# Windowed attention, a gated MLP and routed experts on one core: another way to take exponentials in six banks, and a new order

## The chip, the cores and the metric

The kernel runs on one core of a Trainium2 chip. The core has a matrix engine (TensorE: PE in the profile, with PEld for its weight loads), VectorE (DVE), ScalarE (ACT), GpSimd (POOL), and SyncE (SP), which here issues the loads and stores. The engines run their own queues of instructions in order and wait for one another by semaphores. The metric is the device time of one execution in microseconds.

## The reference

Three stages in float32, each fed with the result of the one before. Batch is 4, the sequence 576, the model width 512.

```python
# 1: 8 heads of 64, causal, window of 64 keys
scores = q @ k.T / 8;  masked outside 0 <= row - col < 64
attn = exp(scores - max);  attn / (attn.sum() + 1e-9) @ v
# 2: gated MLP with a product along the sequence
h = maximum(x @ w_in, 0);  u, v = h[..., :512], h[..., 512:]
v_n = (v - mean) / sqrt(var + 1e-6)
x = (u * (w_spatial @ v_n + b_spatial)) @ w_out
# 3: four causal attention experts, the best two of each token
out = sum over chosen e of w_e * softmax(x wq[e] (x wk[e]).T / 8) (x wv[e]) wo[e]
```

## The kernel before, in words

**Planner.** The Python code doesn't write its instructions in a fixed order. It makes nodes: a cost in nanoseconds for each engine that could do it, what it depends on, the buffers that it takes, and a priority. `Planner.run` plays the engines forward in time with these costs, and whenever an engine is free it emits the ready node of the best priority. A node with a choice (a copy, say, on ACT or DVE) goes to the engine that is expected to end it first, with a bias for each engine. So what stands where in the queues follows from tables of numbers at the head of the file: `SWITCH` (a penalty when PE changes between 64-row and 128-row work), `DVE_BIAS`, `POOL_BIAS` and `EFT` (one number for each of the two runs of the planner), and `SHIFT`, which adds an offset to the priority of every unit of work. It runs twice: once for stages 1 and 2 with the preparation of weights for stage 3 ("phase 1", to about 280 us of the trace), once for stage 3 ("phase 2").

**Dummies.** At the start PE multiplies the identity by itself (`heat`), `WARM` times in one go, and then there are `FILL` = 60 single such nodes of the lowest priority, which the planner emits wherever PE has nothing else that is ready. All are executed; in the profile they are `bank<-ident`, two matmul instructions each.

**Attention of stage 1** (`a_couple`). The 48 groups (batch, pair of heads, third of the sequence) go in 24 couples. A couple fills two banks of PSUM, one for each head of its pairs: PE computes scores in 64-row matmuls (`bank<-kt,qa`, or `ut,qa` and `vt`); DVE scales them, adds the mask and takes the row's least value (L546, three pieces of 128x128; signs are turned, so that the least stands for the greatest score); ACT takes three exponentials with the least as bias, each with the sum of the row accumulated (L552); DVE adds a constant to the sums (L568) and takes the reciprocal (L570); POOL, DVE (L560) or ACT (L558) multiplies; PE transposes (L564, `ident,pa`); ACT or DVE copies to `pt`; PE multiplies by the values (`pt,vt` or `pt,woh`).

**Gated MLP.** Weights come as 64-bit floats and are turned into float32 and split in a high and a low part: DVE shifts and joins words (L686 to L696), ACT or POOL copies the high part, POOL or DVE subtracts it to get the low part (`w<-y,w` at L357). The activations `x` are split in the same way (`xh`, `xl`, and `xt` for the last 64 tokens of a batch). A product takes three matmuls, high by high, high by low, low by high. The v half of the first layer is made of 128x512 matmuls (`w,xh`), the u half of 128x288 (`xh,w`). Then come the product along the sequence with `wsp_h` and `wsp_l`, the gate (L835), and `w_out`.

**Stage 3.** For each batch and pair of experts: `qs`, `kd`, `kz` copies, scores with the mask on DVE (L1207), exponentials on ACT (L1218), normalisation together with the gate on DVE or POOL (L1222), transposes on PE (L1238), copies to `pg` on ACT or DVE (L344, L348), products with the values and with `wo` and copies to `ot` for the store.

A helper issues all plain matmuls (L333), another the copies (L344 for ACT, L346 for POOL, L348 for DVE), a third the subtractions (L357).

Of the kernel before, what the change touches and what calls it, by code (L numbers as in the profile page):

```python
# [26 lines left out]
SWITCH = 107920.0  # L27
A_BIAS = 10098.0
C_BIAS = 162315.0
DVE_BIAS = (1136.0, 1147.0)  # L30
POOL_BIAS = (1131.0, 1068.0)
WARM = 8
FILL = 60
LOADS = (-130000, -120000, -43801, -5807, 14591, 18276, 34028)
EFT = (636.0, 778.0)
# [233 lines left out]
def attn_gmlp_moe_kernel(ctx: ExitStack, tc: tile.TileContext, kq0, qT, kT, v, w_in, wspT, b_sp, w_outT,  # L269
# [228 lines left out]
    def a_couple(n0):  # L498
# [25 lines left out]
        def vap(x, vi, e):  # L524
            b, p, _ = grp[x]
            c = e * 64 + (0 if b else (p % 2) * 128)
            return hv[x][:, vi, c:c + 64]

        def s_mm(_):
            for j in range(3):  # L530
                for x, e in ((0, 0), (1, 1), (1, 0), (0, 1)):
                    win = max(0, 64 * (3 * grp[x][2] + j - 1))
                    mm(bank[e][HALF[x], j * 128:(j + 1) * 128], qap(x, j, e), kap(x, win, e))

        def mask(j):
            return MASK[tuple(int(3 * g + j > 0) for _, _, g in grp)]

        S_N[n0] = S_N[n0 + 1] = top = N((PE, 816), s_mm, kn + [Q_N[n0], Q_N[n0 + 1], S_N.get(n0 - 1)], alloc=bank, use=hk, prio=prio,
                                        form=1)
        done = []  # L540
        for ps, pt in zip(bank, pts):
            pa, mx, ps2 = r_pa.new(), r_mx.new(), r_at.new()

            def s_top(_, ps=ps, pa=pa, mx=mx):
                for j in range(3):
                    dve.tensor_tensor_reduce(out=pa[:, j, :], in0=ps[:, j * 128:(j + 1) * 128],  # L546
                                             in1=mask(j), scale=-0.125, scalar=3.0e38,
                                             op0=ALU.add, op1=ALU.min, accum_out=mx[:, j, 0:1])
# [24 lines left out]
            done.append(N(on_copy(384), lambda e, pt=pt, ps2=ps2: copy(e, pt.t.rearrange("p a b -> p (a b)"), ps2[:, :384]),
                          [a], use=[ps2, pt], prio=prio))
# [554 lines left out]
    def c_gate(b):  # L1129
# [6 lines left out]
        def gt():  # L1136
            return ga[:, 0]
# [16 lines left out]
        tt, tr_ = dve.tensor_tensor, dve.tensor_reduce
        n1 = N_(90, lambda: tr_(out=m1(0), in_=lg, axis=AX.X, op=ALU.max), LG_N[b], [ex, ga, gb])
# [5 lines left out]
        nf = N_(0, lambda: None, [n2, n3, n4])  # L1161
# [14 lines left out]
    def unit(b, pr, e, I):  # L1176
# [38 lines left out]
        if len(parts) == 2:  # L1215
            tops = [N((DVE, 70), lambda e: dve.tensor_reduce(out=mc[:m, 0:1], in_=mc[:m, 0:2], axis=AX.X, op=ALU.min), tops, use=[mc], prio=prio)]
# [211 lines left out]
```

## Time and profile before

| | us |
|---|---|
| time before, median of 2 runs (447.51 to 447.91) | 447.71 |
| the profiled execution: its time | 448.94 |
| its span in the trace | 447.1 |
| busy in the span: PE | 438.9 (98%), 3962 instructions |
| DVE | 310.9 (70%), 1241 |
| ACT | 293.1 (66%), 926 |
| POOL | 107.4 (24%), 154 |
| granted clock of PE, mean | 1.0 |

The profiled execution is longer than its span by 448.94 - 447.1 = 1.84 us, which lie ahead of its first and behind its last instruction. Times of a row in order of time are the start from the beginning of the span and the duration; "x6" counts the instructions that the row joins. Matmuls are pipelined, so their durations overlap and the pitch (start to start) says what one costs. What stands in brackets is idle time ahead of the row and the instruction that ended it.

### The profile page before, as it was taken

How to read it: one execution, taken by the hardware profiler on the slowest of the kernel's cores; microseconds unless marked ns; L12 is line 12 of the kernel's file. 1: busy time of each engine (PE TensorE's matmuls, PEld its weight loads, DVE VectorE, ACT ScalarE, POOL GpSimd, SP SyncE). 2: the span in 40 equal slices, each digit the busy share in tenths (PEclk: the TensorE clock that was granted, in tenths of full speed). 3: DMA queues.
4: the chain of work that ended last, by engine and by line, in shares of the span. 5: the costliest groups of instructions: out<-in, count | busy, mean ns of one | idle time of the engine just before them, and what ended most of it. 6: DMA issues, size and time to landing. Idle time of an engine off the chain costs nothing.

```text
span 447.1 us, 10829 instructions
## 1 busy us (share of the span) xinstructions
PE 438.9 (98%) x3962; PEld 396.0 (89%) x3962; DVE 310.9 (70%) x1241; ACT 293.1 (66%) x926; POOL 107.4 (24%) x154
## 2 busy tenths in 40 slices
PE   8999999999999999999999999999999999999996
PEld 7977899989899879998899999789899978897875
DVE  4989989962875988024544556998697987787650
ACT  4989989662676969203322346987675978777863
POOL 4335782400310126000200251610031011011110
PEclk9999999999999999999999999999999999999999
DMA  7994837140242605003001000000010001000114
GB/s 280 281 330 122 251 101 221 45 140 0 64 138 64 179 7 144 0 1 95 1 1 48 0 1 1 1 2 1 1 48 25 1 2 48 0 2 25 71 53 160
DMA packets 31079, 33.10 MB, mean 74 GB/s; under 512 B 1905, under 2 KB 24689, under 8 KB 31026
## 3 DMA queue, kind: packets, MB, share of 16 engines
q1 hardware_dynamic: 31026, 32.41, 23.4%
q8 instruction: 31, 0.51, 0.5%
q14 instruction: 22, 0.18, 0.1%
HBM read 27.68 MB, written 4.72 MB: 72 GB/s over the span
## 4 chain that ended last, share of the span: by engine, by line
PE 87%; DVE 6%; ACT 4%; issue 2%; POOL 1%; POOLq 0%; ACTq 0%; DVEq 0%
PE bank L333 79%; PE bank L1238 5%; PE bank L564 3%; DVE p L1207 1%; ACT pa L552 1%; DVE qs L357 1%; POOL p L1222 1%; DVE p L1222 1%; ACT p L1218 1%; DVE pa L546 0%; ACT pa L558 0%; DVE pa L560 0%; DVE kz L357 0%; ACT pg L344 0%; ACT kd L344 0%
## 5 line engine op out<-in xcount | busy, mean ns | idle before, releaser
L333 PE MATMUL bank<-xh,w 128*128 128x288 f32 x512 | 109.6, 298 | 0.0
L333 PEld LDWEIGHTS bank<-xh,w 128*128 128x128 f32 x512 | 84.1, 188 | 0.9 <-DVE st L767 0.2
L333 PE MATMUL bank<-xl,w 128*128 128x288 f32 x256 | 75.3, 294 | 0.0
L333 PE MATMUL bank<-w,xh 128*128 128x512 f32 (+1 forms) x256 | 64.7, 342 | 0.2 <-ACT pt L344 0.2
L552 ACT ACTIVATE pa<-pa,mx 128x128 f32<-128x128 f32 x144 | 55.9, 400 | 5.4 <-DVE mx L546 5.4
L333 PEld LDWEIGHTS bank<-xl,w 128*128 128x128 f32 x256 | 48.2, 188 | 0.4
L333 PEld LDWEIGHTS bank<-w,xh 128*128 128x128 f32 x256 | 43.2, 188 | 5.7 <-ACT pt L344 0.5
L1218 ACT ACTIVATE p<-p,mc 128x128 f32<-128x128 f32 (+4 forms) x72 | 41.8, 582 | 8.4 <-DVE mc L1207 7.7
L1222 POOL TENSOR_SCALAR p<-p,mc,fx 128x256 f32<-128x256 f32 (+4 forms) x26 | 17.1, 658 | 111.3 <-DVE mc L1221 52.2
L333 PE MATMUL bank<-w,xl 128*128 128x512 f32 (+1 forms) x128 | 43.2, 338 | 0.0
L333 PE MATMUL bank<-wsp_h,vh 128*128 128x288 f32 x128 | 38.6, 302 | 0.0
L333 PE MATMUL bank<-wsp_h,vl 128*128 128x288 f32 x128 | 37.7, 295 | 0.0
L333 PE MATMUL bank<-wsp_l,vh 128*128 128x288 f32 x128 | 37.7, 294 | 0.0
L1207 DVE CUSTOM_DVE_ANT_0 p<-bank,cmask 128x128 f32<-128x128 f32 (+4 forms) x72 | 33.2, 482 | 5.2 <-PE bank L333 4.2
L770 POOL TENSOR_TENSOR st<-st,nhalf 128x1 f32<-128x1 f32 (+1 forms) x20 | 12.3, 615 | 98.7 <-DVE st L769 98.7
L344 ACT ACTIVATE pg<-bank 128x128 f32<-128x128 f32 (+4 forms) x71 | 29.1, 440 | 5.2 <-PE bank L1238 4.7
L546 DVE CUSTOM_DVE_ANT_0 pa<-bank,mask 128x128 f32<-128x128 f32 x120 | 28.4, 284 | 5.9 <-POOL mx L415 4.1
L1238 PE MATMUL bank<-ident,p 128*128 128x128 f32 x192 | 30.1, 278 | 1.5 <-POOL p L1222 0.7
L333 PE MATMUL bank<-kd,qs 128*128 128x128 f32 (+5 forms) x96 | 30.5, 335 | 0.0
L552 ACT ACTIVATION_READ_ACCUMULATOR pa<-pa,mx 128x1 f32 x144 | 28.6, 199 | 0.0
L333 PE MATMUL bank<-kz,qs 128*128 128x128 f32 (+5 forms) x96 | 28.4, 313 | 0.0
L835 DVE TENSOR_TENSOR y<-bank,ut 128x288 f32<-128x288 f32 x24 | 10.9, 454 | 24.9 <-PE bank L333 24.9
(209 smaller groups left out, 1083.4 us busy)
## 6 DMA issues: line engine op xcount, KB each, us to landing
vt<-in_v_dram SPq DMA_DIRECT2D x12, 512.0 KB, 4.9
qa<-in_qT_dram SPq DMA_DIRECT2D x44, 96.0 KB, 3.8
out_dram<-ot SPq DMA_DIRECT2D x15, 256.0 KB, 2.0
y<-in_w_in_dram SPq DMA_DIRECT2D x7, 512.0 KB, 7.3
kt<-in_kT_dram SPq DMA_DIRECT2D x12, 288.0 KB, 5.0
y<-in_w_outT_dram SPq DMA_DIRECT2D x4, 512.0 KB, 4.5
y<-in_wspT_dram SPq DMA_DIRECT2D x2, 576.0 KB, 4.2
vt<-in_kq_dram SPq DMA_DIRECT2D x2, 384.0 KB, 4.4
```

The costliest lines, as they stand in the source:

```text
L333: pe.matmul(o, lhsT, rhs, start=start, stop=stop)
L344: act.activation(o, i, AF.Copy)
L357: engs[e].tensor_tensor(out=o, in0=a, in1=hi.bitcast(F32), op=ALU.subtract)
L546: dve.tensor_tensor_reduce(out=pa[:, j, :], in0=ps[:, j * 128:(j + 1) * 128], in1=mask(j), scale=-0.125, scalar=3.0e38, op0=ALU.add, op1=A ...
L552: act.activation(pa[:, j, :], pa[:, j, :], AF.Exp, bias=mx[:, j, 0:1], scale=-1.0, accum_out=mx[:, j, 1:2])
L564: pe.transpose(ps2[:, j * 128:(j + 1) * 128], pa[:, j, :], ident)
L770: a = N((POOL, 464), lambda e: pool.tensor_tensor(out=st[:m, 9:10], in0=st[:m, 8:9], in1=nhalf[:m], op=ALU.pow), [n1], use=[st])
L835: dve.tensor_tensor(out=o, in0=ps[:, :HS], in1=u[:, d, tk], op=ALU.mult)
L1207: dve.tensor_tensor_reduce(out=P[:, a0:a1], in0=ps[:, :w], in1=msk, scale=-0.125, scalar=3.0e38, op0=ALU.add, op1=ALU.min, accum_out=mc[:, ...
L1218: a = N((ACT, 284 + 0.87 * L), lambda e: act.activation(P[:m, :L], P[:m, :L], AF.Exp, bias=mc[:m, 0:1], scale=-1.0, accum_out=mc[:m, 2:3]) ...
L1222: a = N({POOL: 328 + 0.832 * L, DVE: 90 + 0.52 * L}, lambda e: engs[e].tensor_scalar(P[:, :L], P[:, :L], mc[:, 3:4], fx[:, I, ev:ev + 1], ...
L1238: pe.transpose(ps[:, j * m:(j + 1) * m], P[:, j * 128:(j + 1) * 128], ident)
```

## The change

In the first six couples (`n0 < 12`), the second of the two banks (`i == 1`) no longer takes its exponentials in three pieces with accumulation. The row's least value is subtracted first, for all three pieces at once, by POOL or DVE; then ACT takes one exponential of 128x384; then DVE sums the three pieces with one reduction. The rest of the chain stays. Behind it, the numbers of the planner are new (costs of two nodes, the biases, `WARM` 8 to 4, all three `SHIFT` tables), some nodes are marked as using SBUF on both sides for the planner's model, and so the order differs nearly everywhere. Line numbers behind the new code are higher by 9 or so: L568 becomes L577, L570 L579, L686 L695, L1222 L1232.

```diff
-SWITCH = 107920.0
+SWITCH = 133946.30139722134
-DVE_BIAS = (1136.0, 1147.0)
-POOL_BIAS = (1131.0, 1068.0)
-WARM = 8
+DVE_BIAS = (1041.5841120727002, 2147.197231178334)
+POOL_BIAS = (957.1946613242204, 230.99823993453649)
+WARM = 4
 FILL = 60
-EFT = (636.0, 778.0)
+EFT = (557.6301780703249, 3908.0839196396537)
 SHIFT = (
-    {0: -120449, 1: -48640, 2: 516074,
...
+    {0: 685473, 1: 922898, 2: -2911782,
...
-        S_N[n0] = S_N[n0 + 1] = top = N((PE, 816), s_mm,
+        S_N[n0] = S_N[n0 + 1] = top = N((PE, 816 if n0 else 1500), s_mm,
...
-        for ps, pt in zip(bank, pts):
+        for i, (ps, pt) in enumerate(zip(bank, pts)):
...
             a = N((DVE, 606), s_top, [top], alloc=[pa, mx], use=[ps], prio=prio)
-            a = N((ACT, 1160), s_exp, [a], use=[pa, mx], prio=prio)
+            if n0 < 12 and i == 1:
+                a = N({POOL: 955, DVE: 468}, lambda e, pa=pa, mx=mx: engs[e].tensor_tensor(
+                    out=pa.t, in0=pa.t, in1=mx[:, :, 0:1].to_broadcast([128, 3, 128]), op=ALU.subtract),
+                      [a], use=[pa, mx], prio=prio, sbuf=True)
+                a = N((ACT, 440), lambda e, pa=pa: act.activation(pa.t, pa.t, AF.Exp, scale=-1.0), [a], use=[pa], prio=prio)
+                a = N((DVE, 470), lambda e, pa=pa, mx=mx: dve.tensor_reduce(out=mx[:, :, 1], in_=pa.t, axis=AX.X, op=ALU.add),
+                      [a], use=[pa, mx], prio=prio)
+            else:
+                a = N((ACT, 1160), s_exp, [a], use=[pa, mx], prio=prio)
...
-            a = N({POOL: 1053, DVE: 450, ACT: 880}, s_norm, [a], use=[pa, mx], prio=prio, sbuf=True)
+            a = N({POOL: 955, DVE: 468, ACT: 880}, s_norm, [a], use=[pa, mx], prio=prio, sbuf=True)
```

**DVE, the first couple.** The difference of DVE's queue behind the score reductions of the first couple's two banks (`mx_122` and `mx_123`); L546 are the score reductions, L569 is the new subtraction, L573 the new sum.

```order
 L546 ISA pa,mx_123<-bank_68,mask_87 128x128
 L546 ISA mx_123 128x1
-L568 TENSOR_REDUCE mx_122<-mx_122 128x3
+L569 TENSOR_TENSOR pa<-pa,mx_123 128x384
+L577 TENSOR_REDUCE mx_122<-mx_122 128x3
+L579 RECIPROCAL mx_122<-mx_122 128x3
+L573 TENSOR_REDUCE mx_123<-pa 128x3
 L546 ISA pa,mx_124<-bank_69,mask_82 128x128
 L546 ISA mx_124 128x1
```

The subtraction for the second bank now follows the reductions at once, and the new sum stands ahead of the next couple's first reduction (`mx_124`).

**PE, ahead of the first u group.** The queue of before from the end of a score group (`kt,qa`) over a v group (`w,xh`) to the first u matmuls (`xh,w`, 128x288); `w,xt` is the v product for the last tokens.

```order
L333 MATMUL bank_68<-kt,qa 64x128
L333 MATMUL bank_73<-w,xh 128x512 x2
L333 MATMUL bank_73<-w,xl 128x512
...
L333 MATMUL bank_71<-w,xt 128x512
L333 MATMUL bank_72<-xh,w 128x288
L333 MATMUL bank_72<-xl,w 128x288
```

The queue of after, up to the same u matmuls; between the marks lie more of one score group.

```order
L333 MATMUL bank_73<-kt,qa 64x128
L333 MATMUL bank_66<-pt,woh 64x64 x12
L333 MATMUL bank_67<-kt,qa 64x128
L333 MATMUL bank_72<-kt,qa 64x128
...
L333 MATMUL bank_72<-kt,qa 64x128
L564 MATMUL bank_70<-ident,pa 128x128 x3
L333 MATMUL bank_68<-xh,w 128x288
L333 MATMUL bank_68<-xl,w 128x288
```

The v group and the `xt` group now follow later; a group of weighted sums (`pt,woh`), a score group and three transposes stand ahead of the u matmuls instead.

**DVE, the last weight for the first u group.** The queue of after; `w<-y_721,w` is the last low part of the four u weights, and `y_721` its float32 value.

```order
L705 SCALAR_TENSOR_TENSOR y_721<-bank_70,y_721 128x512
L777 TENSOR_SCALAR st<-st 128x1
L778 TENSOR_SCALAR st<-st 128x1
L577 TENSOR_REDUCE mx_122<-mx_122 128x3
L577 TENSOR_REDUCE mx_123<-mx_123 128x3
L357 TENSOR_TENSOR w<-y_610,w 128x512
L357 TENSOR_TENSOR w<-y_721,w 128x512
L781 TENSOR_SCALAR vr<-vr,st 128x512
L357 TENSOR_TENSOR xl<-bank_66,xh 128x192
```

Two subtractions for weights follow each other here, behind the small steps of two banks' sums (L577, L579).

**SP, the first loads.** The queue of before, then that of after; `vt`, `ut`, `woh` and `wol` hold the first keys, queries and values, `w_` and `y_` the words of `w_in`.

```order
L426 DMA vt<-in_kq_dram 128x768 x2
L426 DMA w_149<-in_w_in_dram 128x1024
L426 DMA woh<-in_v_dram 128x2x256
L426 DMA y_152<-in_w_in_dram 128x1024
L426 DMA y_154<-in_w_in_dram 128x1024
L426 DMA y_156<-in_w_in_dram 128x1024
L426 DMA wol<-in_v_dram 128x2x256
L426 DMA qa<-in_qT_dram 128x192 x2
L426 DMA ut<-in_kT_dram 128x4x256
```

```order
L426 DMA vt<-in_kq_dram 128x768 x2
L426 DMA wol<-in_v_dram 128x2x256
L426 DMA qa<-in_qT_dram 128x192 x2
L426 DMA woh<-in_v_dram 128x2x256
L426 DMA w_150<-in_w_in_dram 128x1024
L426 DMA y_165<-in_w_in_dram 128x1024
L426 DMA y_167<-in_w_in_dram 128x1024
L426 DMA y_169<-in_w_in_dram 128x1024
L426 DMA woh<-in_v_dram 128x3x256
L426 DMA qa<-in_qT_dram 128x192 x2
L426 DMA ut<-in_kT_dram 128x4x256
```

Values and queries come ahead of the four `w_in` loads now, and `ut` comes behind one more load of values (384 KB) and the others that moved up.

**The rest of the order.** Four dummies that stood alone between groups far behind the opening are gone, and all 64 stand ahead of the first u group, as 64 of the 68 did before. In phase 2 more copies from PSUM and fewer of the normalisations stand on DVE, and fewer copies on ACT.

## Rows read from the trace of the kernel before

**Rows 1.** Waits of PE: engine, line, releaser; total us, times, longest

```profile
PE bank L564 <- DVE pa L560: 0.9, 1, 0.9
...
PE bank L564 <- ACT pt L344: 0.5, 1, 0.5
```

**Rows 2.** Busy time by stretch; PEclk, DMA share and GB/s stand last

```profile
7.09:26.00 18.91, 18.02 (x254) 16.40 (x252) 17.65 (x80) 18.39 (x73) 5.89 (x10) 1.00 0.98 324
26.00:47.60 21.60, 20.91 (x271) 17.24 (x272) 19.88 (x85) 19.28 (x73) 10.32 (x11) 1.00 0.68 206
...
53.40:280.00 226.60, 226.60 (x2172) 212.10 (x2171) 140.12 (x516) 124.35 (x410) 52.14 (x71) 1.00 0.22 65
280.00:430.00 150.00, 148.43 (x1100) 130.54 (x1100) 123.77 (x508) 117.94 (x335) 29.01 (x35) 1.00 0.06 21
```

**Rows 3.** PE in order of time: start us, us, instruction, count

```profile
47.00 0.92 PE L333 MATMUL bank<-pt,vt 128*64 128x64 f32 x24
47.85 0.89 PE L333 MATMUL bank<-kt,qa 64*64 64x128 f32 x24
48.66 0.73 PE L333 MATMUL bank<-w,xh 128*128 128x512 f32 x2
...
51.54 2.01 PE L333 MATMUL bank<-w,xt 128*128 128x512 f32 x8
53.39 0.29 PE L333 MATMUL bank<-xh,w 128*128 128x288 f32 x1
```

**Rows 4.** The same, around three late dummies

```profile
200.04 0.49 PE L333 MATMUL bank<-ident 128*128 128x128 f32 x2
200.37 0.82 PE L564 MATMUL bank<-ident,pa 128*128 128x128 f32 x6
201.12 0.92 PE L333 MATMUL bank<-pt,vt 128*64 128x64 f32 x24
...
203.23 0.49 PE L333 MATMUL bank<-ident 128*128 128x128 f32 x2
203.47 0.70 PE L333 MATMUL bank<-w,xh 128*128 128x512 f32 x2
```

**Rows 5.** DVE in order of time, the opening; idle and its releaser in brackets

```profile
7.09 0.29 DVE L546 CUSTOM_DVE_ANT_0 pa<-bank,mask 128x128 f32<-128x128 f32 x1 [4.12 <-POOL mx L415]
...
23.45 1.48 DVE L560 TENSOR_TENSOR pa<-pa,mx 128x384 f32<-128x384 f32 x1
...
26.88 0.56 DVE L560 TENSOR_TENSOR pa<-pa,mx 128x384 f32<-128x384 f32 x1
```

**Rows 6.** POOL in order of time, the opening

```profile
23.25 1.27 POOL L357 TENSOR_TENSOR w<-y,w 128x512 fp32r<-128x512 f32 x1 [2.82 <-ACT w L344]
27.08 1.05 POOL L560 TENSOR_TENSOR pa<-pa,mx 128x384 f32<-128x384 f32 x1 [2.56 <-DVE mx L570]
```

**Rows 7.** ACT in order of time, the opening

```profile
7.42 0.40 ACT L552 ACTIVATE pa<-pa,mx 128x128 f32<-128x128 f32 x1 [5.41 <-DVE mx L546]
...
7.82 0.39 ACT L552 ACTIVATE pa<-pa,mx 128x128 f32<-128x128 f32 x1
...
41.93 0.99 ACT L558 ACTIVATE pa<-pa,mx 128x128 f32<-128x128 f32 x3 [0.25 <-DVE mx L568]
```

**Rows 8.** Groups of instructions: busy us, mean ns, idle before

```profile
L1222 DVE TENSOR_SCALAR p<-p,mc,fx 128x128 f32<-128x128 f32 (+4 forms) x46 | 25.0, 543 | 1.1
...
L568 DVE TENSOR_REDUCE mx<-mx 128x3 f32<-128x6 f32 x48 | 6.9, 151 | 1.1 <-ACT pa L552 0.6
...
L348 DVE CAST xh<-y 128x576 fp32r<-128x576 f32 x4 | 4.2, 1064 | 0.0
...
L348 DVE COPY pg<-bank 128x384 f32<-128x384 f32 (+4 forms) x9 | 3.9, 433 | 1.7 <-PE bank L1238 1.0 <-PE bank L1255 0.6
```

**Rows 9.** ACT in order of time, the end

```profile
438.18 0.38 ACT L344 ACTIVATE ot<-bank 128x256 f32<-128x256 f32 x1 [0.33 <-PE bank L333]
...
443.68 0.60 ACT L344 ACTIVATE ot<-bank 128x512 f32<-128x512 f32 x1 [0.78 <-PE bank L333]
```

More of the change, by code (lines that the diff above doesn't have):

```diff
@@ L536, in mask @@
             return MASK[tuple(int(3 * g + j > 0) for _, _, g in grp)]
-        S_N[n0] = S_N[n0 + 1] = top = N((PE, 816), s_mm, kn + [Q_N[n0], Q_N[n0 + 1], S_N.get(n0 - 1)], alloc=bank, use=hk, prio=prio,
+        S_N[n0] = S_N[n0 + 1] = top = N((PE, 816 if n0 else 1500), s_mm, kn + [Q_N[n0], Q_N[n0 + 1], S_N.get(n0 - 1)], alloc=bank, use=hk, prio=prio,
                                         form=1)
         done = []
-        for ps, pt in zip(bank, pts):
+        for i, (ps, pt) in enumerate(zip(bank, pts)):
             pa, mx, ps2 = r_pa.new(), r_mx.new(), r_at.new()
@@ L1149, in lead, with N_ @@
             return m1(n)[:, :, None].to_broadcast(s3)
-        def N_(c, f, deps, alloc=()):
-            return N((DVE, c), lambda e: f(), deps, alloc=alloc, use=[] if alloc else [ex, ga, gb])
+        def N_(c, f, deps, alloc=(), sbuf=True):
+            return N((DVE, c), lambda e: f(), deps, alloc=alloc, use=[] if alloc else [ex, ga, gb], sbuf=sbuf)
         tt, tr_ = dve.tensor_tensor, dve.tensor_reduce
-        n1 = N_(90, lambda: tr_(out=m1(0), in_=lg, axis=AX.X, op=ALU.max), LG_N[b], [ex, ga, gb])
+        n1 = N_(90, lambda: tr_(out=m1(0), in_=lg, axis=AX.X, op=ALU.max), LG_N[b], [ex, ga, gb], False)
         n2 = N_(155, lambda: tt(out=gt(), in0=lf, in1=le, op=ALU.is_gt), [n1])
@@ L1160, in c_gate @@
         n4 = N((ACT, 210), lambda e: act.activation(ex.t, ex.t, AF.Exp), [n4], use=[ex])
-        nf = N_(0, lambda: None, [n2, n3, n4])
+        nf = N_(0, lambda: None, [n2, n3, n4], sbuf=False)
         n2 = N_(155, lambda: tt(out=gt(), in0=gt(), in1=eq(), op=ALU.add), [n2, n3])
-        n2 = N_(150, lambda: tr_(out=rk(), in_=gt(), axis=AX.X, op=ALU.add), [n2])
+        n2 = N_(150, lambda: tr_(out=rk(), in_=gt(), axis=AX.X, op=ALU.add), [n2], sbuf=False)
         n2 = N_(80, lambda: dve.tensor_scalar(rk(), rk(), 1.5, None, op0=ALU.is_lt), [n2])
         n2 = N_(90, lambda: tt(out=ex.t, in0=ex.t, in1=rk(), op=ALU.mult), [n2, n4])
-        n2 = N_(90, lambda: tr_(out=m1(1), in_=ex.t, axis=AX.X, op=ALU.add), [n2])
+        n2 = N_(90, lambda: tr_(out=m1(1), in_=ex.t, axis=AX.X, op=ALU.add), [n2], sbuf=False)
         n2 = N_(70, lambda: dve.tensor_scalar(m1(1), m1(1), 1e-9, None, op0=ALU.add), [n2])
-        n2 = N_(75, lambda: dve.reciprocal(m1(1), m1(1)), [n2])
+        n2 = N_(75, lambda: dve.reciprocal(m1(1), m1(1)), [n2], sbuf=False)
         n4 = N_(90, lambda: tt(out=ex.t, in0=ex.t, in1=lead(1), op=ALU.mult), [n2])
@@ L1215, in unit @@
         if len(parts) == 2:
-            tops = [N((DVE, 70), lambda e: dve.tensor_reduce(out=mc[:m, 0:1], in_=mc[:m, 0:2], axis=AX.X, op=ALU.min), tops, use=[mc], prio=prio)]
+            tops = [N((DVE, 75), lambda e: dve.tensor_reduce(out=mc[:m, 0:1], in_=mc[:m, 0:2], axis=AX.X, op=ALU.min),
+                      tops, use=[mc], prio=prio)]
         a = N((ACT, 284 + 0.87 * L), lambda e: act.activation(P[:m, :L], P[:m, :L], AF.Exp, bias=mc[:m, 0:1], scale=-1.0,
```

6 rows, old and new, of the table SHIFT are left out of this document.

## Prediction

> **What bounds the kernel now.** I read the waits of TensorE first. Its matmul engine (PE) waits for others at only a few places, and apart from the start the two longest single ones lie in the opening: 0.9 us for a norm on DVE and 0.5 us for ACT's copy of transposed weights [rows 1]. The windows say the same by stage [rows 2]. From 53.40 to 280.00 PE is busy for 226.60 of 226.60 us, so nothing that another engine saves there is worth anything. From 7.09 to 26.00 it is busy 18.02 of 18.91, from 26.00 to 47.60 it is 20.91 of 21.60: idle 0.89 and 0.69, together 1.58, which is those two waits and a little more. From 280.00 to 430.00 it is 148.43 of 150.00, idle 1.57. The granted clock is 1.00 throughout, so there is no slow stretch to win back. The kernel is PE bound, and what is left to gain is (a) those two idles of 1.6 us each, (b) PE work that computes nothing (the dummy matmuls), (c) the ends of the span.
>
> But PE being busy in the opening is partly an appearance: the planner lays dummy matmuls wherever no real group is ready. With 64 dummies ahead of the first u group ("U1", the first 128x288 matmul, at 53.39 [rows 3]), a late DVE or ACT shows up as dummies ahead of a group, not as idle. So I ask in this stage when U1 can start, by PE's queue and by DVE's, since from there to 280 PE runs without a gap.
>
> **The change, part by part.**
>
> *Four warm-up dummies.* There are 68 dummies before and 64 after. Before, four of them stand late, between groups at 172 to 203 us, inside the stretch where PE is full; after, none does. Two have pitches in the timeline: 200.04 to 200.37, and 203.23 to 203.47, so 0.33 and 0.24 [rows 4]; four at their mean of 0.28 are **-1.1 us**. If what they covered there was a real wait, it reappears and the gain is 0. I take -1.1, since the stage is full of other ready work. The start gains nothing: the first score reduction on DVE begins at 7.09 after a wait for POOL's memsets [rows 5], and these are unchanged.
>
> *U1.* Ahead of it both orders hold 64 dummies, but the new order moves real groups behind it. One v group is gone (48.66 to 51.54, 2.88), the `xt` group too (51.54 to 53.39, 1.85), two weighted-sum groups of 0.85 (47.00 to 47.85), and six transposes (six of them take 200.37 to 201.12, 0.75); one score group is added (47.85 to 48.66, 0.81) [rows 3, 4]. That is 2.88 + 1.85 + 1.70 + 0.75 - 0.81 = 6.37, so U1 would stand at 53.39 - 6.37 = 47.02 with the same waits, and at 47.02 - 1.6 = 45.4 if these waits vanish. The work moved is done later, so only a shift against 47.02 counts in the sum.
>
> DVE sets the other bound. U1's weights end with `w<-y_721,w`. Up to that row the new order gives DVE the same amount of work as the old one had done by 47.6: there it was busy for 17.65 + 19.88 = 37.5 of the 40.5 us [rows 2]. What the change adds to DVE in that stretch is nearly what the order moves behind it, so at the old pace the last weight is ready near 47.6, and U1 lies between 45.4 and 47.6. I take the middle, 46.5: **-0.5 us** against 47.02.
>
> *The six banks.* In each, three exponentials with accumulation on ACT (pitch 7.42 to 7.82, 0.40, so 1.2) become one of 128x384. The trace has none; three 128-wide scalings without accumulation take 0.99 in a row [rows 7], a bound from above, and one 128-wide piece is 0.40, a bound from below; I take 0.45, nearer to the single piece because it is one instruction. ACT saves 6 x 0.75 = 4.5 us. DVE gets the sum over 128x384: between 0.15 for the small sum at L568 [rows 8] and 0.56 for a multiply on the same tile (26.88 [rows 5]); I take 0.5, since it reads as many elements: 3.0 us. The subtraction has the form of the norm at L560. Three go to POOL at 1.05 each (27.08 [rows 6]) and three to DVE at 0.56, or 1.48 where POOL works at the same time (23.45 [rows 5], with POOL's 1.27 at 23.25 [rows 6]): 1.7 to 4.4 us. The new chain of a bank (0.56, 0.45, 0.5) is 1.5 against 1.2 and the small sum, no shorter. All of it lies beside PE's dummies and the other groups, and the DVE sum above holds it. So at the level of PE it costs nothing of its own; its cover gone, it is priced by the U1 bounds and the second rival.
>
> *Loads.* On SP's queue the first `ut` load stands behind 576 KB more. At the 324 GB/s of 7.09 to 26.00, where the DMA share is 0.98 [rows 2], that is 1.8 us. The score groups that need it stand behind a run of 17 dummies, some 4.8 us at 0.28, so nothing is added.
>
> *Phase 2.* The new biases put 29 more copies on DVE and as many fewer on ACT; a copy of `pg` is 0.433 and a norm 0.543 [rows 8], and five norms leave DVE, as do two wide casts of 1.064 [rows 8]. 29 x 0.433 - 5 x 0.543 - 2 x 1.064 = 7.7, so about +8 us on DVE, which is busy 123.77 of 150.00 [rows 2]. At 132 of 150 it still has 18 us free; the cost lies between -1.57 (the idle vanishes) and +8 (every copy on the path). I take 0: PE waits for either engine's copies in the same way, and ACT gets as much lighter.
>
> *Tail.* ACT's last copy is 0.60 for 512 columns; the new order ends with 256 columns, 0.38 [rows 9]: -0.2.
>
> **Sum.** -1.1 - 0.5 + 0 + 0 - 0.2 = -1.8. The profiled execution has 448.94 us with a span of 447.1; the median is 447.71, 1.2 below it. I apply the sum to the median: **445.9 us**.
>
> **The rivals.**
>
> *A, every wait vanishes.* Both idles go: -1.1 - 1.6 - 1.57 - 0.2 = -4.5, so 443.2. For it: DVE and ACT have slack in phase 2 [rows 2], and ACT is 4.5 us lighter in the opening. Against: DVE's pace in the opening is not shorter. Condition: U1 at 45.4 or earlier.
>
> *B, DVE becomes the bound of the opening (slower).* Three subtractions on DVE stand among POOL's weight subtractions, which POOL has more of. If each takes 1.48 instead of 0.56, DVE is 3 x 0.92 = 2.8 us later: U1 at 47.6 + 2.8 = 50.4, 3.4 after 47.02. Sum -1.1 + 3.4 - 0.2 = +2.1: 449.8. It decides for slower from U1 later than 47.02 + 1.3 = 48.3. For it: the rows of 1.48 and 1.27 that overlap [rows 5, 6]. Against: the norm at 26.88 takes 0.56 although POOL begins one of its own at 27.08, inside it [rows 5, 6].
>
> The Trainium skill (SBUF — State Buffer, "Who interferes with whom") says that a DVE instruction with two SBUF inputs and a GpSimd instruction that reads SBUF share a port pair, and that the one which came first holds it to its end, while a reduction on DVE does not contend. The trace agrees for the first half, with 1.48 beside 0.56; no row here shows a wide reduction. By that rule alone the subtractions would bring rival B's 449.8 if all three met POOL, and the six sums would stay out of it.
>
> *C, phase 2 turns DVE bound.* All of +8 on the path: 447.71 - 1.8 + 8 = 453.9; half of it 449.9. For it: DVE is the busiest after PE. Against: 18 us still free.
>
> *D, the change does nothing.* The exponentials were not on the path, and the four dummies covered waits that come back: 447.7.
>
> **How the numbers follow.** Forecast (444.4 to 447.2) 0.48; A 0.20; B 0.14; C 0.08; D 0.10. The likeliest, 445.9, is the prediction. The range of 442.0 to 451.0 takes in A with 1 us below it for ends that I price too high, B, and half of C; it leaves out the rest of C and odd ends. About 2% (9 us) is what a measurement of this kernel can tell from no change. No case reaches 438.8: faster 0.02. Only C with something more passes 456.7: slower 0.04. Same 0.94.
>
> **What would show it.** U1 at 46 to 47 in the new profile; no dummy after it; PE idle under 1.6 us between 7.09 and U1; DVE subtractions at 0.56, sums at 0.5, exponentials at 0.45; in phase 2 PE idle between 1 and 2 us with DVE near 132. I am wrong if U1 stands later than 48.3, if the waits of the last groups of phase 2 grow past 3 us, or if new waits show up between 53 and 280, where I price everything at nothing.

## The result, and the profile after

The changed kernel takes 453.17 us (453.09 to 453.25) where the kernel before takes 447.71: the ratio is 1.0121, with an interval of 1.0097 to 1.0146. It is 5.5 us slower. I had predicted 445.9, with a range of 442.0 to 451.0, so both the sign and the range are wrong. The profiled execution has 453.09 us and a span of 451.3.

Busy time by stretch of the kernel after, with the columns of [rows 2]:

```profile
7.09:26.00 18.91, 18.82 (x258) 16.97 (x258) 18.24 (x82) 14.82 (x49) 8.28 (x13) 1.00 1.06 346
26.00:47.60 21.60, 21.20 (x284) 17.82 (x284) 19.86 (x85) 20.98 (x73) 12.79 (x14) 1.00 0.74 219
47.60:53.40 5.80, 4.82 (x54) 4.42 (x48) 5.51 (x33) 5.33 (x22) 4.19 (x5) 1.00 0.59 217
53.40:280.00 226.60, 225.29 (x2139) 208.89 (x2137) 138.41 (x522) 120.95 (x405) 58.25 (x82) 1.00 0.21 61
280.00:430.00 150.00, 148.41 (x1082) 129.94 (x1082) 126.68 (x509) 105.72 (x293) 30.79 (x38) 1.00 0.06 22
```

The kernel before, in the stretch that [rows 2] leave out:

```profile
47.60:53.40 5.80, 5.80 (x57) 4.48 (x53) 5.75 (x41) 5.80 (x25) 5.08 (x5) 1.00 0.87 238
```

Ahead of 47.60 PE is idle for 0.09 + 0.40 = 0.49 us, where [rows 2] gave 1.58: the waits of the opening went, as the first two lines show. Others are there behind it: 0.98 us of idle between 47.60 and 53.40, and 1.31 between 53.40 and 280, where the kernel before had none. From 280 to 430 PE is as busy as before (148.41 against 148.43). These two windows don't hold the same work, since phase 2 begins about 1.1 us later in the kernel after. Over the whole of phase 2, from the last matmul of the gated MLP to PE's last, the work is the same. The kernel after, then the kernel before:

```profile
262.21:446.94 184.73, 183.04 (x1333) 160.08 (x1331) 143.65 (x578) 125.42 (x343) 37.39 (x58) 1.00 0.07 24
```

```profile
261.13:443.20 182.07, 180.50 (x1333) 159.67 (x1331) 137.57 (x552) 135.00 (x382) 33.09 (x45) 1.00 0.07 24
```

The same 1,333 matmuls take 2.66 us more, and PE's idle time has grown only from 1.57 to 1.69: nearly all of the loss stands in the profile as busy time of PE.

PE's waits in the kernel after (engine, line, releaser; total us, times, longest):

```profile
PE bank L333 <- DMA kt<-in_kT_dram: 1.0, 1, 1.0
...
PE bank L333 <- ACT ut L352: 0.7, 1, 0.7
PE bank L1248 <- DVE kz L357: 0.4, 1, 0.4
PE bank L564 <- POOL pa L560: 0.4, 1, 0.4
PE bank L333 <- DVE xt L357: 0.3, 1, 0.3
```

The 0.9 us for the norm and the 0.5 us for `pt` of [rows 1] are gone, and in phase 1 new waits stand in their place, by a load (`kt`), ACT (`ut`), POOL (`pa`) and DVE (`xt`); the line of L1248 belongs to phase 2. In order of time on PE, with the idle time ahead in brackets:

```profile
45.29 0.55 PE L564 MATMUL bank<-ident,pa 128*128 128x128 f32 x3 [0.40 <-POOL pa L560]
45.59 0.38 PE L333 MATMUL bank<-xh,w 128*128 128x288 f32 x1
...
48.96 0.40 PE L333 MATMUL bank<-xh,w 128*128 128x288 f32 x1 [0.70 <-ACT ut L352]
...
51.76 0.40 PE L333 MATMUL bank<-xh,w 128*128 128x288 f32 x1 [0.28 <-DVE xt L357]
...
78.02 1.53 PE L333 MATMUL bank<-kt,qa 64*64 64x128 f32 x46 [1.01 <-DMA kt<-in_kT_dram]
...
82.74 0.38 PE L333 MATMUL bank<-wsp_h,vh 128*128 128x288 f32 x1 [0.24 <-DVE mx L577]
```

U1 stands at 45.59, where [rows 3] have 53.39. One wait is ahead of it, and four come behind it, up to the first product along the sequence (`wsp_h,vh`, at 82.74, "the mix" from here). A wait costs more in pitches than the idle time in brackets: the excess of these four pitches over the size that the same groups have elsewhere is about 2.8 us behind U1 (0.76, 0.35, 1.28 and 0.39, an estimate from the rows), of which 2.29 are idle time.

The groups of the new operations (busy us, mean ns, idle before), and the norms of phase 2 for [rows 8]:

```profile
L569 DVE TENSOR_TENSOR pa<-pa,mx 128x384 f32<-128x384 f32 x3 | 1.7, 558 | 0.1
...
L569 POOL TENSOR_TENSOR pa<-pa,mx 128x384 f32<-128x384 f32 x3 | 2.5, 830 | 5.7 <-DVE mx L546 5.7
...
L572 ACT ACTIVATE pa<-pa 128x384 f32<-128x384 f32 x6 | 3.2, 526 | 0.7 <-DVE pa L569 0.4 <-POOL pa L569 0.3
L573 DVE TENSOR_REDUCE mx<-pa 128x3 f32<-128x384 f32 x6 | 3.3, 544 | 0.3 <-ACT pa L572 0.3
...
L1232 DVE TENSOR_SCALAR p<-p,mc,fx 128x128 f32<-128x128 f32 (+4 forms) x41 | 20.4, 499 | 1.0
```

Subtraction 0.558 on DVE and 0.830 on POOL, exponential 0.526, sum 0.544: I had 0.56 (or 1.48 beside POOL), 1.05, 0.45 and 0.5.

To say where the 5.5 us are, I cut each trace at the starts of three instructions of PE: U1, the last `w,woh` matmul of the gated MLP (128x256, "end of phase 1") and PE's last matmul. One `w,wol` matmul still follows the second of them, 0.12 us later in every trace, and "phase 2" is counted from that one. "Tail" is from the start of PE's last matmul to the end of the span.

| kernel | U1 | end of phase 1 | phase 2 | tail | span |
|---|---|---|---|---|---|
| before | 53.39 | 261.01 | 182.07 | 3.94 | 447.1 |
| after | 45.59 | 262.09 | 184.73 | 4.38 | 451.3 |
| before, late dummies left out | 52.12 | 258.52 | 182.02 | 3.95 | 444.6 |

The profiled execution before was itself 1.2 us above the median, and that lies in its opening: in four other profiles with the same opening U1 stands at 52.02 to 52.91. So the third row is the fair one beside after, since neither has a late dummy. The difference is 3.57 in phase 1, 2.71 in phase 2, 0.43 in the tail, 6.7 in all; the late dummies give back 1.4 (their own run is below). That makes +5.3, and 5.5 were measured.

### The profile page after: what moved, and what is told of

The parts are those of the page before. It is cut to its first block, busy times and chain, and to the rows that moved or that the text cites. A ratio compares the mean times of both kernels' runs of the same rounds, so it can differ in the third digit from the quotient of the medians.

```text
span 451.3 us, 10805 instructions
## 1 busy us (share of the span) xinstructions
PE 441.2 (98%) x3954; PEld 395.6 (88%) x3954; DVE 318.1 (70%) x1269; ACT 279.5 (62%) x864; POOL 121.3 (27%) x176
## 4 chain that ended last, share of the span: by engine, by line
PE 82%; DVE 10%; POOL 3%; issue 3%; ACT 1%; POOLq 0%; ACTq 0%; DVEq 0%
PE bank L333 74%; PE bank L1248 5%; PE bank L564 3%; DVE pa L546 1%; DVE p L1216 1%; DVE kz L357 1%; DVE xl L357 1%; DVE t1v L357 1%; POOL p L1232 0%; DVE pa L560 0%; DVE qs L357 0%; DVE p L1232 0%; ACT pt L344 0%; POOL w L346 0%; POOL vr L781 0%
## 5 line engine op out<-in xcount | busy, mean ns | idle before, releaser
L1232 POOL TENSOR_SCALAR p<-p,mc,fx 128x384 f32<-128x384 f32 (+4 forms) x31 | 20.0, 650 | 133.4 <-ACT p L1228 21.9
L552 ACT ACTIVATE pa<-pa,mx 128x128 f32<-128x128 f32 x126 | 49.1, 401 | 6.9 <-DVE mx L546 6.9
L779 POOL TENSOR_TENSOR st<-st,nhalf 128x1 f32<-128x1 f32 (+1 forms) x20 | 13.4, 668 | 102.4 <-DVE st L778 99.1
L1216 DVE CUSTOM_DVE_ANT_0 p<-bank,cmask 128x512 f32<-128x512 f32 (+4 forms) x72 | 32.8, 480 | 0.6 <-PE bank L333 0.3
L1248 PE MATMUL bank<-ident,p 128*128 128x128 f32 x192 | 30.4, 279 | 1.5 <-POOL p L1232 0.8
L546 DVE CUSTOM_DVE_ANT_0 pa<-bank,mask 128x128 f32<-128x128 f32 x120 | 28.3, 282 | 4.7 <-POOL mx L415 4.1
L333 PE MATMUL bank<-kd,qs 128*128 128x384 f32 (+5 forms) x96 | 30.3, 334 | 0.2 <-DVE mc L1216 0.2
L333 PE MATMUL bank<-kz,qs 128*128 128x384 f32 (+5 forms) x96 | 28.1, 313 | 0.0
L1248 PEld LDWEIGHTS bank<-ident,p 128*128 128x128 f32 x192 | 22.0, 140 | 6.9 <-POOL p L1232 2.0
L333 PEld LDWEIGHTS bank<-w,xl 128*128 128x128 f32 x128 | 24.1, 188 | 2.8
```

The lines of the kernel that those rows point to most:

```text
L333: pe.matmul(o, lhsT, rhs, start=start, stop=stop)
L779: a = N((POOL, 464), lambda e: pool.tensor_tensor(out=st[:m, 9:10], in0=st[:m, 8:9], in1=nhalf[:m], op=ALU.pow), [n1], use=[st])
L1216: dve.tensor_tensor_reduce(out=P[:, a0:a1], in0=ps[:, :w], in1=msk, scale=-0.125, scalar=3.0e38, op0=ALU.add, op1=ALU.min, accum_out=mc[:, ...
L1232: a = N({POOL: 328 + 0.832 * L, DVE: 90 + 0.52 * L}, lambda e: engs[e].tensor_scalar(P[:, :L], P[:, :L], mc[:, 3:4], fx[:, I, ev:ev + 1], ...
L1248: pe.transpose(ps[:, j * m:(j + 1) * m], P[:, j * 128:(j + 1) * 128], ident)
```

## The experiments

In all of them the planner's order and its choice of engines are written into the kernel as a list, so that an edit changes what it says and nothing else. Times in brackets are the lowest and the highest of a kernel's runs; the kernel before ran beside each, at 447.8 to 448.1.

**The exponentials apart from the order.** First the new order with the old exponentials:

```diff
-    lambda e: engs[e].tensor_tensor(out=pa.t, in0=pa.t, in1=mx..., op=ALU.subtract)
+    lambda e: None
-    lambda e: act.activation(pa.t, pa.t, AF.Exp, scale=-1.0)
+    s_exp
-    lambda e: dve.tensor_reduce(out=mx[:, :, 1], in_=pa.t, ...)
+    lambda e: None
```

> The order of the changed kernel, instruction for instruction, but the six banks take their three exponentials with accumulation as before (no subtraction ahead, no wide sum behind; the queues hold nothing in their places). Theory O (the order costs the time, the six banks do not): 453.2 within 1 us. Theory X (the subtraction, the wide exponential and the sum cost the time): back by most of 5.5 us, below 450. If ACT bounds the opening in this order, 6 x 0.75 = 4.5 us more on ACT appear as up to 457.

It took 455.52 us (455.16 to 457.54), ratio 1.0176 [1.0156, 1.0196]: slower still than the change, by 2.35. That is the third case of the expectation, at about half of its 4.5 us.

```profile
47.81 0.55 PE L564 MATMUL bank<-ident,pa 128*128 128x128 f32 x3 [0.45 <-POOL pa L560]
48.26 0.40 PE L333 MATMUL bank<-xh,w 128*128 128x288 f32 x1
```

U1 is at 48.26 instead of 45.59, 2.67 later, and the end of phase 1 at 264.84 instead of 262.09, 2.75 later. Between 5 and 50 us DVE now waits four times for ACT's exponentials before it can add up a bank's sums (L576, which is L577 in the kernel after, where there is one such wait of 0.2 for the small sums and one of 0.3 for the wide ones):

```profile
DVE mx L576 <- ACT pa L552: 2.0, 4, 0.8
```

So with three exponentials in each bank ACT makes DVE late in the opening of the new order, and PE waits for what comes behind. Then the old order with the new exponentials, all six subtractions on DVE:

```diff
 def s_top(...):
     ... (three reductions)
+    if wide: dve.tensor_tensor(out=pa.t, in0=pa.t, in1=mx..., op=ALU.subtract)
 def s_exp(...):
+    if wide: return act.activation(pa.t, pa.t, AF.Exp, scale=-1.0)
+ if wide: dve.tensor_reduce(out=mx[:, :, 1], in_=pa.t, ...)   # ahead of L568
```

> The order of before, instruction for instruction, but the six banks subtract first (all six on DVE, right behind the score reductions), take one exponential, and sum on DVE. Theory O: 447.7 within 1 us, since dummies cover 6 x 0.75 us less on ACT and 6 x 1.1 us more on DVE. Theory X: 450 or more, most of the 5.5 us. A third way, DVE bounds the opening: 447.7 + up to 6.6 less what idles there, with U1 (the first u group) later than 53.39.

450.92 us (450.68 to 451.47), ratio 1.0066 [1.0054, 1.0078], so +3.0: DVE bounds the opening, the third case again, at under half of its 6.6. PE's waits, and the window of the opening:

```profile
PE bank L568 <- DVE pa L564: 3.0, 3, 1.5
```

```profile
26.00:47.60 21.60, 20.10 (x222) 16.65 (x224) 21.05 (x93) 17.23 (x59) 9.94 (x12) 1.00 0.54 167
```

DVE is busy 21.05 of 21.60 us and PE waits three times for its norms; U1 goes to 55.26, 2.4 to 3.2 behind its usual 52.02 to 52.91. Nearly the same edit is worth -2.35 in one order and +3.0 in the other. It isn't quite the same, since POOL takes three of the six subtractions in the new order and DVE takes all six here; how much of the 3.0 comes from those three, no run separates. The edit takes work from ACT and gives work to DVE, and what that is worth depends on which of the two PE waits for.

**The late dummies alone.** The kernel before, with the four late dummies left out:

```diff
-FILL = 60
+FILL = 56    # the order without the four late ones
```

> The kernel of before, all queues in its order, without the four dummies that stand late between groups (FILL 56, the four left out of the order). Theory L (they cover nothing): 447.9 - 1.1 = 446.8. Theory C (they cover waits, which come back): 447.9. The dummies' bank is free for others from 44 us on instead of 203, with no change in the order.

446.59 us (446.35 to 447.80, 10 runs), ratio 0.9969 [0.9959, 0.9979]: -1.4, and no wait of PE behind U1 in phase 1. Nothing was hidden under these dummies. This kernel is faster than the kernels before and after.

**One half new, one half old.** The list of phase 1 from one kernel, that of phase 2 from the other:

```diff
-ORDER = (new_phase_1, new_phase_2)
+ORDER = (new_phase_1, old_phase_2)
```

> Phase 1 (attention and MLP) in the order of the changed kernel, phase 2 (experts) in the order of before. From the two traces: the changed kernel is 1.3 us later at the end of phase 1 and loses another 2.9 in phase 2 and the tail. Theory S (the loss is shared as the traces say): 449.0 within 0.7. Theory P1 (all of it hangs on phase 1, phase 2 only passes it on): 452 to 453.5. Theory P2 (all in phase 2): 447.7.

450.49 us (449.88 to 453.36), ratio 1.0072 [1.0048, 1.0096]: 1.5 more than I expected, because I had taken the loss of phase 1 from the profile before with its late opening. Its trace has 262.10 for the end of phase 1, as after (262.09), and 182.16 for phase 2, as before (182.07). The halves don't act on each other here, and each has a loss of its own.

```diff
-ORDER = (old_phase_1, old_phase_2)
+ORDER = (old_phase_1, new_phase_2)
```

> The mirror: phase 1 in the order of before, phase 2 in the order of the changed kernel. Theory S: 450.6 within 0.7 (2.9 us more than before). Theory P1: 447.7. Theory P2: 452 to 453.5, the whole loss.

454.04 us (453.54 to 454.37), ratio 1.0133 [1.0120, 1.0146], against 450.6 expected. This join brought a cost that neither kernel has. PE at the seam:

```profile
263.20 0.50 PE L333 MATMUL bank<-w,zt 128*128 128x260 f32 x2 [1.39 <-POOL zt L346]
263.88 0.39 PE L333 MATMUL bank<-w,zt 128*128 128x260 f32 x1 [0.18 <-POOL zt L357]
264.51 1.59 PE L333 MATMUL bank<-w,zt 128*128 128x260 f32 x9 [0.24 <-POOL zt L346]
265.89 0.44 PE L333 MATMUL bank<-xh,w 128*128 128x288 f32 x1
266.13 0.44 PE L333 MATMUL bank<-xl,w 128*128 128x288 f32 x1
```

PE waits three times for POOL, 1.8 us in all, and then a 128x288 matmul has a pitch of 0.24 us (265.89 to 266.13) where it is 0.13 elsewhere (49.20 to 49.33 in the kernel after, for one). The granted clock had fallen there, as the last section shows. Phase 2 takes 188.44 instead of 184.73. So this run is no measure of phase 2; the one before it is.

**Phase 1: which of the waits behind U1 is the cause?** The longest is for the load of `kt`. I gave its ring a third buffer and moved the load forward on SP, ahead of the loads of `vt`, `w_outT` and `qa` (to make room, a mask tile takes over a tile that is no longer needed):

```diff
-r_kt = ring(p1, "kt", [128, S], F32, 2)
+r_kt = ring(p1, "kt", [128, S], F32, 3)    # and its load ahead of those of vt, w_outT, qa
```

> The changed kernel in its own order, but kt has a third buffer (paid for by letting one of the mask tiles reuse the tile of indices), and the load of keys that PE waits for at 78.02 (1.0 us by the waits, 1.25 by the pitch of that group) is issued some 5 us earlier on SP's queue. Theory W (the waits behind U1 add to the end, since PE is full from there to 280): 453.2 - 1.2 = 452.0. Theory G (given back: what waited there waits for something else next): 453.2, no change.

453.24 us (452.83 to 453.73), ratio 1.0119 [1.0105, 1.0133]: no gain. The wait for the load is gone, and three others have grown or are new:

```profile
PE bank L564 <- POOL pa L560: 1.3, 1, 1.3
PE bank L333 <- DVE mx L577: 0.9, 1, 0.9
...
PE bank L333 <- DVE xl L357: 0.7, 1, 0.7
```

The first is ahead of U1, which stands at 46.51 in this profile instead of 45.59, so part of its lateness is not behind U1 at all. From U1 to the mix it takes 36.84 us instead of 37.15: of the load's 1.0 us, 0.3 came through, and the rest stood ahead of a late DVE. The second suspect was ACT's copy of `ut`, which stands behind four casts of other weights. I moved these behind it:

```diff
 # order of ACT: t1w, t1w, t2w and the wsp_h, wsp_l chain behind the copy of ut
-(t1w, t1w, t2w, wsp_h, ut)
+(ut, wsp_h, ..., t1w, t1w, t2w)
```

> The changed kernel in its own order, but on ACT the four copies of the weights of the product along the sequence (t1w twice, t2w, wsp_h; 2.8 us from 45.40 to 48.6) go behind the eviction of ut (L352) and later work; one low part on POOL moves behind two others. PE's queue is unchanged. Theory W: the wait for ut at 48.96 (0.7 us) goes, and part of the 0.5 us for xt at 51.76: 453.2 - 0.7 to 1.2 = 452.0 to 452.5. Theory G: 453.2.

454.88 us (454.72 to 455.06), ratio 1.0156 [1.0142, 1.0170]: slower by 1.7. The wait for `ut` is gone, and PE waits for DVE instead, 1.3 us for `pt`, 1.0 for `xt` and 1.0 for `mx` ahead of the mix, which now stands at 84.42. So it is DVE that is late between U1 and the mix. What it does there in the kernel after, up to the mix, then the same subtraction for the second batch, and POOL beside the first:

```profile
76.02 1.49 DVE L348 CAST t1v<-vr 64x512 fp32r<-64x512 f32 x1
...
79.41 2.36 DVE L357 TENSOR_TENSOR t1v<-vr,t1v 64x512 fp32r<-64x512 f32 x1
...
131.59 0.68 DVE L357 TENSOR_TENSOR t1v<-vr,t1v 64x512 fp32r<-64x512 f32 x1
```

```profile
78.70 2.52 POOL L357 TENSOR_TENSOR wol<-y,woh 128x512 fp32r<-128x512 f32 x2
```

One subtraction of 512 columns takes 2.36 us, through both of POOL's; for the second batch, with POOL idle, it takes 0.68. The small steps that the mix waits for (L577, from 81.81 on) stand right behind it. I left this one instruction out for the first batch (so the low part of `t1v` is left at zero there), with the early load:

```diff
-lambda e: sub(e, t1v[64:128], vr[:64], t1v[0:64])
+lambda e: sub(e, t1v[64:128], vr[:64], t1v[0:64]) if b else None
```

> As x5 (third kt buffer, its load early), and DVE leaves out one operation: the low part of the last 64 tokens of v in the first batch (t1v, 2.4 us at 80.0 in x5, stalled by POOL's two low parts of w_out that run at the same time); that half of the tile is set to zero at the start instead, so a small part of the first batch's values is left out. In x5 the wait for keys went, but the first product along the sequence then waited 1.1 us more for DVE. Theory W2 (DVE is the bound up to the first product along the sequence; taking 2.4 us off it lets x5's gain through): the product's wait goes, 453.2 - 1.0 = 452.2. Theory G (something else is next): 453.2 within 0.4.

452.05 us (451.72 to 452.71), ratio 1.0092 [1.0078, 1.0105], where the early load alone had 453.24 and the kernel after 453.17. The mix has no wait ahead of it. U1 stands at 45.48, so the kernel after (45.59) is the one to compare the trace with: the mix is at 81.61 instead of 82.74 and phase 1 ends at 260.80 instead of 262.09. From U1 to the mix it takes 36.13 us, 1.02 less than in the kernel after and 0.71 less than with the early load alone. So DVE's work there bears on the end of phase 1, and the load and one stalled instruction are over 1 us of it. PE still waits 1.94 us in this stretch, the longest for `ut` (1.0) and for DVE's `xl` (0.7).

**Phase 2: the engines or PE's order?** Each node of phase 2 takes the engine that it has in the other kernel, and PE's order stays:

```diff
-ORDER[1] = [(node, new engine, time), ...]
+ORDER[1] = [(node, old engine, time), ...]
```

> The changed kernel with PE's queue as it is, but in phase 2 each copy and each normalisation is done by the engine that did it before (22 copies of pg go back from DVE to ACT, 23 normalisations from POOL to DVE, 18 from DVE to POOL, and a dozen narrow ones). Theory D (DVE's load costs the 2.6 us that phase 2 lost): phase 2 falls from 184.7 to 182.1 and the time to 450.5. Theory F (the order of PE's groups costs them: more entries into pg groups, more matmuls right behind transposes): 453.2 within 0.7.

456.69 us (456.44 to 457.37), ratio 1.0198 [1.0184, 1.0212]. Then the old order of phase 2 with the new engines for the copies and norms:

```diff
-ORDER[1] = [(node, old engine, time), ...]
+ORDER[1] = [(node, new engine, time), ...]    # copies and norms
```

> The mirror: the kernel of before, all queues' order as before, but in phase 2 the copies and normalisations are done by the engines that do them in the changed kernel (those of the first weights of phase 2 stay). Theory D: 447.9 + 2.6 = 450.5. Theory F: 447.9 within 0.7.

456.00 us (454.94 to 456.96), ratio 1.0180 [1.0160, 1.0199]. Neither of the expected cases came in either run. PE's waits in this one:

```profile
PE bank L1238 <- POOL p L1222: 2.0, 3, 1.3
PE bank L333 <- DVE pg L348: 1.9, 1, 1.9
PE bank L1238 <- DVE p L1222: 1.7, 1, 1.7
```

Either crossing makes new waits and takes some 3 us more than the changed kernel. They show that an order and its engines belong together, and nothing on which of them costs the 2.7 us. A smaller edit, the engines of four of the first norms and of one wide cast in phase 2 as in the old order:

```diff
-# four norms: one on POOL, three on DVE; one cast of 576 columns on POOL
+# four norms: one on DVE, three on POOL; that cast on DVE
```

> The changed kernel, PE's queue unchanged, but the first four normalisations and the first wide cast of phase 2 are done by the engines of before (three norms back to POOL, one and the cast to DVE). In the changed kernel DVE's norms at 283.22 and 284.17 take 0.84 and 0.67 while POOL casts, and PE then waits 0.57 at 285.2 and 0.41 at 286.4. Theory W2: both waits go, phase 2 falls from 184.75 to 183.8 and the time to 452.2. Theory G: 453.2, the waits move.

453.61 us (453.39 to 453.74), ratio 1.0123 [1.0108, 1.0138], the same as after. Its phase 2 took 185.25. Of the two waits aimed at, the one for `kz` at 285.84 (0.41) is gone; the one for `mc`, 0.16 in the kernel after, has grown to 0.56, and another came at 294.15:

```profile
286.11 0.50 PE L333 MATMUL bank<-kd,qs 128*128 128x512 f32 x1 [0.56 <-DVE mc L1216]
294.15 0.98 PE L1248 MATMUL bank<-ident,p 128*128 128x128 f32 x7 [0.45 <-POOL p L1232]
```

**Phase 2: blocks of `pg,v`.** Since the loss is booked as busy time, I looked for something in which the two orders differ and which no wait shows. The products with the values (`pg,v`) write 64 rows of a bank each, in two halves, and the pitches at both ends of such a block are long. The old order has 13 blocks of them and the new one 16, since three pairs are torn apart. So I tore three pairs apart in the old order, and changed nothing else:

```diff
 # PE's order in phase 2, at three places (T a transpose or a score group)
-pg,v  pg,v  T
+pg,v  T  pg,v
```

> The kernel before with its order written out, and one thing changed in phase 2: in three places where two groups of 64-row products (pg,v) follow each other directly on PE, the next other group is put between them, so that 16 blocks of such products stand there as in the new order, in place of 13; no engine choice is changed. Theory B (part of phase 2's 2.6 us is what PE pays to enter and leave these blocks): entering and leaving took 0.22 to 0.27 and 0.09 us in the profile before, so three more blocks are 0.7 to 1.1 us; the time from the end of phase 1 to PE's last matmul grows from 182.07 to 182.8 to 183.2, and the kernel from 447.9 to 448.6 to 449.0. Theory N (blocks cost nothing of their own, the 2.6 us are waits): 182.1, 447.9. If a product that comes later makes a copy late, a wait of PE for it shows up at one of the three places and is to be taken off.

449.40 us (448.97 to 449.82), ratio 1.0034 [1.0020, 1.0048]: +1.5, or 0.4 above what I had expected at most. Phase 2 took 183.05 instead of 182.07, +0.98, as expected; in three profiles of the old order it took 182.02 to 182.16. The rest of the +1.5 is not in phase 2. The longest waits of PE in phase 2 are those of the kernel before:

```profile
PE bank L1238 <- POOL p L1222: 0.7, 3, 0.3
PE bank L1238 <- DVE mc L1220: 0.5, 1, 0.5
```

So three more blocks cost 1.0 us by the trace, some 0.33 each, with no wait to show for it. If they cost as much in the new order, which no run tests, that is over a third of phase 2's 2.7. The Trainium skill (TensorEngine Tiling (Array Packing), "Key Properties") states that changing the tiling mode drains TensorE. That the price of a block comes from there is not shown, and matmuls of 64 columns alone don't bring it: in the score groups of the kernel after they stand among those of 128 columns at the same pitch of 0.13.

```profile
343.11 0.29 PE L333 MATMUL bank<-kd,qs 128*64 128x288 f32 x1
343.24 0.29 PE L333 MATMUL bank<-kz,qs 128*64 128x288 f32 x1
343.37 0.29 PE L333 MATMUL bank<-kd,qs 128*128 128x288 f32 x1
```

## Why the prediction was wrong, point by point

**Late dummies, -1.1: right.** -1.4 [-1.8, -0.9] when it was done alone.

**U1 at 46.5: within its bounds, and of no worth.** U1 came at 45.59, between 45.4 and 47.6 but 0.9 earlier than the middle that I took; DVE had the last weight ready at 45.79, not at 47.6. And I subtracted the moved work from 53.39, and this profile was 0.5 to 1.4 us late in its opening; from 52.02 to 52.91 the same 6.37 gives 45.65 to 46.54, so U1 gained next to nothing on the work that was moved. The -0.5 was the lateness of one execution. I had seen that it was 1.2 above the median, and put the gap at no place.

**"From there to 280 PE runs without a gap": the step that failed.** It was true of the old order, and I carried it over to the new one, whose queue behind U1 I had not priced. New waits between 53 and 280 were my own sign of being wrong, and they came. The stretch from U1 to the mix, in the kernel before (with, first, the time that this stretch takes up in the kernel after) and then in the kernel after:

```profile
45.59:82.74 37.15, 37.15 (x427) 34.57 (x422) 33.68 (x131) 32.04 (x110) 23.75 (x22) 1.00 0.57 178
53.39:70.27 16.88, 16.88 (x217) 15.89 (x216) 13.91 (x46) 15.08 (x44) 12.84 (x12) 1.00 0.39 132
```

```profile
45.59:82.74 37.15, 34.86 (x425) 30.04 (x424) 35.00 (x145) 32.03 (x119) 25.98 (x27) 1.00 0.57 173
```

Before, it is 16.88 us long, PE is full and DVE busy for 13.91, 82%. The new order brings U1 forward and puts the mix back, mostly by moving work between them: the stretch holds 425 matmuls instead of 217 and is 37.15 us, with DVE busy for 35.00 (94%), ACT for 32.03 and PE idle for 2.29. The busy share alone doesn't make the waits: in the same 37.15 us the old order has DVE busy for 33.68 (91%), and PE is never idle. What has changed is which steps PE stands in front of. With little slack on DVE, and no dummy left to fill in (the last one ahead of U1 stands at 31.07), a late step is a wait of PE. I had asked of each group that moved behind U1 whether it costs something there, and never who feeds it. That is my rival B's mechanism, DVE as the bound, at a place where I didn't look: B decided by U1 being later than 48.3, and U1 was early. That DVE is late there is shown by the early load, the moved `ut` and the omitted subtraction; that it is alone in this is not, since PE's wait for ACT's `ut` stays in the last of the three. Of the 3.6 us of phase 1, 1.3 went with that subtraction and the load; the rest was not taken apart further.

**DVE stalls beside POOL.** I had priced them for the new subtractions. There they did not come: 0.558 us each for the three on DVE, as clean as 26.88 in [rows 5]. They came at the subtraction of `t1v` at 79.41, 2.36 us instead of 0.68 beside two of POOL's, over 40 us behind the last of the six (35.71 to 36.54, on POOL). The Trainium skill (SBUF — State Buffer, "Who interferes with whom") has the rule that I had cited: the one of two that came first holds the port pair to its end. The trace agrees with it for POOL's first subtraction, which began at 78.70. DVE then also stood through the second, which came after DVE's own start, and ended 0.55 us behind it; that goes beyond the rule as I cited it. And I had applied it only to what the diff names.

**Six banks at 0: wrong, in both directions.** The durations were right within 0.08 us, but for POOL's subtraction (0.830 against 1.05). But -2.35 in the new order and +3.0 in the old one are no zero: the cover that I named, dummies and other groups, was thinner than the edit. In the old order six subtractions and six sums are about 7.0 us of DVE (six at a mean of 0.615, one of them 0.90, and six of 0.544), and 3.0 of it came through.

**Loads at 0: right for `ut`,** for whose load PE never waits. The later wait for `kt` (1.0) was new, and worth nothing by itself.

**Phase 2 at 0: +2.7.** My bounds of -1.57 and +8 hold it, but I argued about DVE's load alone, and DVE is at 126.68 of 150, not at 132: the norms fell from 25.0 us [rows 8] to 20.4. Rival C, with PE waiting for DVE, is therefore not what happened: idle time is 0.1 of the 2.7. The step that failed is the reading of PE's busy share as a full engine, with idle time as the only price of an order; a long pitch at the start or end of a group counts as busy. Three more blocks are 1.0, if their price carries over. What the remaining 1.7 comes from is not settled: the waits at 285.84 (0.41) and 286.44 (0.16) are new, but others went, and the three runs on the engines each put new waits in the place of old ones.

**Tail, -0.2: wrong sign, +0.4.** The last copy is short, as I said. But the stores queue on SP. ACT in the kernel after, and SP:

```profile
447.30 0.38 ACT L344 ACTIVATE ot<-bank 128x256 f32<-128x256 f32 x1 [0.33 <-PE bank L333]
```

```profile
447.02 1.70 SPq L426 DMA_DIRECT2D out_dram<-ot  x3
```

The copy ends at 447.68, and SP is busy with issues until 448.72; before, the copy of 443.68 [rows 9] ends at 444.28 and SP issues its store at once:

```profile
444.30 0.33 SPq L426 DMA_DIRECT2D out_dram<-ot  x1
```

From the end of the copy to the end of the span it is 3.64 us after and 2.86 before. The new order sends more of its stores at the very end, which I had read from the order and not priced. This is read from the rows; no run tests it.

## What to carry to other kernels

When a new order brings one milestone forward, price the stretch up to the next one too, engine by engine: work pulled ahead of the first is owed to the second, and where fillers ran out, each late step is a wait. An edit that moves work between two engines can have one price in one order and the opposite in another, by which engine is waited for there, so try it alone in the old order before a new order is searched around it. Compare the busiest engine's time over the same work as well as its waits, since what it pays between groups of matmuls is booked as busy, and take the offset of a profiled execution against the median to a place before subtracting from its rows.

## What the runs showed of the hardware that was not expected

PE's granted clock fell after waits in the middle of the kernel, in two runs. In the run with the old phase 1 and the new phase 2 PE waited 1.39, 0.18 and 0.24 us between 261.8 and 264.5, and then the window reads:

```profile
265.90:269.00 3.10, 3.10 (x15) 3.10 (x15) 1.29 (x6) 0.89 (x3) 1.44 (x4) 0.50 0.00 0
269.00:272.00 3.00, 3.00 (x25) 3.00 (x25) 1.07 (x3) 1.20 (x3) 0.00 (x0) 0.99 0.00 0
```

The granted clock (third from the end) is 0.50, the lower of its two levels, for 3 us, and is back at 0.99 in the next 3 us; 15 matmuls lie in the first window and 25 in the second. In the run with the new engines in the old phase 2 it was 0.55 from 335.0 to 338.8, behind a single wait of 1.94, and 0.54 from 410.0 to 413.7, behind one of 1.68. At the pitches of the two levels (0.24 and 0.13 us) the 15 matmuls of the first window lost some 1.5 us, an estimate, after 1.8 us of waits. The length of a wait doesn't decide it: with the old engines in the new phase 2 PE waited 2.33 us for the load of `kt`, up to 79.30, and the clock stayed at its higher level:

```profile
79.30:82.50 3.20, 3.20 (x54) 2.73 (x55) 3.14 (x10) 1.84 (x8) 2.84 (x3) 1.00 0.66 183
```

What decides it, no run here shows. In the changed kernel itself the clock stays at 1.00 up to 430: none of its 5.5 us up to there come from the clock.
